# z^T for the gated block: turned by VectorE and read back through DRAM, in place of TensorE transposes

## The chip, the core and the metric

The kernel runs on one core of a Trainium2 chip. The metric is the device time of one execution in microseconds (us); times of several executions are given as a median. The engines are named as in the profile: PE is TensorE, PEld its weight loads, DVE is VectorE, ACT is ScalarE, POOL is GpSimd, SP is SyncE, which issues most of the loads.

## What is computed

A row block x of 2048 x 512 (float32) goes through four layers, each added to its input:

```
for layer in range(4):
    n = layernorm(x)
    if layer % 2 == 0:                       # mix: real part of a 2-D DFT
        a, b = n @ hid_re.T, n @ hid_im.T
        x = x + seq_re @ a - seq_im @ b
    else:                                    # gated block, F = 1792
        x = x + (gelu(n @ w_gate) * (n @ w_up)) @ w_down
```

## The kernel before

**Products.** Every float32 operand is split into a high and a low part (`split`, line 109: ScalarE copies with rounding, VectorE subtracts), and one product is three matmuls (`mm3`, lines 142 to 146: high by high, high by low, low by high). The larger products are done with seven half-size products in place of eight, in the scheme of Strassen and Winograd; the names A11 to A22, S1 to S4, B11 to B22 and T1 to T4 are those of its blocks and sums.

**SBUF and PSUM.** SBUF is cut into 102 slots of 128 x 512 (`Slots`, line 85), taken from the front of a list and put back at its end; PSUM into 8 tiles. A slot that is taken again waits for the last reader of its earlier content.

**Streamed weights.** The DFT matrices (`ws`, `wh`) and the split w_down (`wd`) come as a list of items in the order of use. `take` (line 221) hands out the next one. Before it does, it splits items up to AHEAD = 5 further on, and `split_next` (line 214) loads up to RAW = 4 beyond that. Loads go to SP's queue. For w_down the item is a pair of loads of halves that are already split, and the "split" does nothing (`lambda *w: w`, line 356).

**Steps on the side.** Work that is not a product is put into a list, `queue` (line 359), and `step` runs one entry after each item of the mix, after each item of the down product, and, while `making` holds, before each product of the gated block. In the first mix the queue first holds the norms and differences of layer 0, and then `down_weight_steps` (line 693) for the 14 pieces of w_down: a load on SP, a split, two stores of the halves on POOL, with two empty steps after each.

The instruction order in the built program is set by a scheduler that works from this order; within an engine the order is fixed then, SP's and POOL's queues too.

**The mix** (`mix`, line 507) goes over four blocks of 512 columns; in each come S2, S3 and A22 products with the sequence matrices and then the products with `wh`, after which a block of x is stored.

**The gated block** (`geglu`, line 728) makes two passes (w = 0, 1) over 1024 rows. A pass needs z^T, the normed rows turned, as eight blocks. `block_steps` (line 441) makes them: `norm(i)` for eight tiles of rows (`normed`, line 368), then for each of four column chunks and two parts `turned` (line 450), which transposes four 128 x 128 pieces on TensorE into a PSUM tile:

```
for i in range(NT):
    nc.tensor.transpose(ps[:, i * P:(i + 1) * P], z[part * NT + i][:, c * P:(c + 1) * P], ident)
```

`first` and `second` copy that tile with ScalarE, split it, and form differences T1, T2, T3. For the first pass these steps are queued at S3 of the last block of the mix (line 606), for the second pass after the first half of the down products of the first (line 876). Before the last stage of a mix everything left in the queue is run.

**Gate and up weights.** In the first pass of layer 1 the 14 pieces of w_gate and w_up are loaded raw (`weight_steps`, line 654: one load of 256 KB, two of 128 KB), summed, split and stored; the load, the sums and four splits are six steps of the queue. Pieces 0 and 1 are made at the end of the mix (lines 593 and 608), piece 2 at the start of the pass (line 860), piece n + 3 after pass n (line 827). Later passes load the split pieces (`weight_load`, line 709).

`up(n, ...)` (line 791) does the seven products of piece n, and between them matmuls of the down product that lags LAG = 6 pieces behind; `down` does the rest of the down products, 12 matmuls an item.

Of the kernel before, what the change touches and what calls it, by code (L numbers as in the profile page):

```python
# [14 lines left out]
P = 128  # L15
# [13 lines left out]
LAG = 6  # L29
EARLY = 2  # L30
# [8 lines left out]
def fnet_geglu(ctx: ExitStack, tc: tile.TileContext, x_in, ws, wh, wgu, wdn, out):  # L39
# [174 lines left out]
    def split_next():  # L214
        n = stream["split"]
        while stream["loaded"] <= min(n + RAW, len(items) - 1):
            load_next()
        parts[n] = items[n][2](*raws.pop(n))
        stream["split"] += 1

    def take():
        n = stream["used"]
        while stream["split"] <= min(n + AHEAD, len(items) - 1):
            need = items[stream["split"]][3]
            if need and need not in cs and stream["split"] > n:
                break
            split_next()
# [10 lines left out]
    def as_is(v):  # L238
        return (v,)

# [112 lines left out]
    for layer in range(0, 4, 2):  # L353
        mix_items(layer)
        for _ in range(NB // 2):
            items.extend((F32R, halves(wds[f]), lambda *w: w, None) for _ in range(2) for f in range(NF))
# [84 lines left out]
    def block_steps(layer, w):  # L441

        z, t = {}, {}

        def norm(i):
            def run():
                z[i] = normed(layer, w * 2 * NT + i)
            return run

        def turned(c, part):  # L450

            ps = ps8.get()
            for i in range(NT):
                nc.tensor.transpose(ps[:, i * P:(i + 1) * P], z[part * NT + i][:, c * P:(c + 1) * P], ident)  # L454
            if c == ND - 1:
                sb.put(*(z.pop(part * NT + i) for i in range(NT)))
            return ps
# [6 lines left out]
        def first(c):  # L464
            def run():
                ps = turned(c, 0)
                t[f"B{1 + c // 2}1", c % 2] = copied(ps)
                blocks[f"B{1 + c // 2}1", c % 2] = split_slot(ps)
                ps8.put(ps)
            return run  # L470

        def second(c):
            def run():
                ps = turned(c, 1)
                if c < 2:
                    t["B12", c] = copied(ps)
                    t["T1", c] = difference(ps, t["B11", c])
                    sb.put(t.pop(("B11", c)))
                else:
                    c0 = c - 2  # L480
                    t["T2", c0] = difference(ps, t["T1", c0])
                    t["T3", c0] = difference(ps, t["B12", c0])
                    sb.put(t.pop(("B12", c0)))
                    blocks["B22", c0] = split_slot(ps)
                ps8.put(ps)
# [14 lines left out]
        one = [norm(i) for i in range(NT)] + [first(c) for c in range(ND)]  # L500
        two = [norm(i) for i in range(NT, 2 * NT)] + [second(c) for c in range(ND)]
        two += [fourth(c) for c in range(2)]
        two += [divide(name, c) for name in ("T2", "T3", "T1", "T4") for c in range(2)]
        return one + two


    def mix(layer):
# [73 lines left out]
        chains, sides, us, ws4 = {}, {}, {}, {}  # L581

        def s2(b):
# [7 lines left out]
            sides[b] = side  # L591
            if last and layer == 0:
                queue.extend(weight_steps(0))
# [8 lines left out]
        def s3(b):  # L602
            last = b == NB - 1
            chain, side, u, w4 = chains[b], sides.pop(b), us.pop(b), ws4.pop(b)
            if last:
                queue.extend(block_steps(layer + 1, 0))
                if layer == 0:
                    queue.extend(weight_steps(1))
# [45 lines left out]
    def weight_steps(n):  # L654
# [36 lines left out]
        return [load, sums] + [divide(i) for i in range(len(pieces))]  # L691

    def down_weight_steps(f):

        raw = []

        def load():
            raw.append(sb.get())
            with tc.issue_after(stream["last"].ins):
                nc.sync.dma_start(raw[0], wdn[f])  # L700

        def store():
            p = plain(raw[0])
            kept(wds[f], p)
            sb.put(*p)

        return [load, store]
# [20 lines left out]
    def geglu(w, layer):  # L728
# [33 lines left out]
        making = layer == 1 and w == 0  # L762
# [28 lines left out]
        def up(n, down):  # L791
            product(n, chain[n], "S2", "T2", False, True)
# [33 lines left out]
            if making and n + 3 < NF:  # L826
                queue.extend(weight_steps(n + 3))
            elif not making and n + 2 < NF:
# [30 lines left out]
        if making:  # L859
            queue.extend(weight_steps(2))  # L860
# [7 lines left out]
        if before_mix:  # L868
# [115 lines left out]
```

## Time and profile before

| | |
|---|---|
| median of 3 runs | 1662.34 us (1661.48 to 1665.74) |
| profiled execution | 1666.76 us |
| its span, first to last instruction | 1664.9 us |
| granted TensorE clock, mean | 0.998 |
| DMA, moved in all | 388.46 MB, 233 GB/s |
| stores by POOL's queue | 57.16 MB |
| instructions | 22527 |

How to read it: a line L144 is line 144 of the kernel; "p" is a PSUM tile, "s" a slot of SBUF, both without their numbers. A group's row gives its count, busy time and mean duration in ns, and then the idle time of the engine before it with what ended it. A row of a windows view gives, for a stretch of the span, the busy time of each engine with the number of instructions, the granted clock and the share of the DMA engines' time. A row of DMA issues gives the count, the size and the median time from issue to landing. In the chain of waits each piece is followed back from the end to what released it.

### The profile page before, as it was taken

How to read it: one execution, taken by the hardware profiler on the slowest of the kernel's cores; microseconds unless marked ns; L12 is line 12 of the kernel's file. 1: busy time of each engine (PE TensorE's matmuls, PEld its weight loads, DVE VectorE, ACT ScalarE, POOL GpSimd, SP SyncE). 2: the span in 40 equal slices, each digit the busy share in tenths (PEclk: the TensorE clock that was granted, in tenths of full speed). 3: DMA queues.
4: the chain of work that ended last, by engine and by line, in shares of the span. 5: the costliest groups of instructions: out<-in, count | busy, mean ns of one | idle time of the engine just before them, and what ended most of it. 6: DMA issues, size and time to landing. Idle time of an engine off the chain costs nothing.

```text
span 1664.9 us, 22527 instructions
## 1 busy us (share of the span) xinstructions
PE 1650.4 (99%) x7296; PEld 1359.2 (82%) x7296; DVE 1190.7 (72%) x2132; ACT 776.2 (47%) x1352; POOL 169.3 (10%) x288
## 2 busy tenths in 40 slices
PE   9999999999999999999999999999999999999999
PEld 6877788888788888888888888888888888888887
DVE  8997978687887765655898785857946556656561
ACT  7744434255565543534663333444635443444440
POOL 3212100021422110000210000000100000100000
PEclk9999999999999999999999999999999999999999
DMA  9788886778766876555665766565695559755551
GB/s 361 247 279 329 306 317 227 253 252 291 273 229 215 292 269 233 172 189 198 216 227 182 240 228 228 168 227 188 225 386 184 171 177 321 259 178 175 186 183 51
DMA packets 200726, 388.46 MB, mean 233 GB/s; under 512 B 23840, under 2 KB 27424, under 8 KB 200608
## 3 DMA queue, kind: packets, MB, share of 16 engines
q1 hardware_dynamic: 183168, 329.86, 59.1%
q0 software_dynamic: 17440, 57.16, 9.1%
q8 instruction: 58, 0.95, 0.2%
q14 instruction: 60, 0.49, 0.1%
HBM read 328.73 MB, written 58.20 MB: 232 GB/s over the span
## 4 chain that ended last, share of the span: by engine, by line
PE 93%; DVE 3%; DMA 2%; issue 1%; ACT 1%; SPq 0%; DVEq 0%; ACTq 0%
PE p L144 31%; PE p L145 30%; PE p L146 30%; DMA s<-wgu 2%; DVE s L111 1%; PE p L551 1%; PE p L454 1%; DVE s L135 1%; DMA s<-ws 1%; DVE s L132 1%; DMA s<-x 0%; DVE s L725 0%; DVE s L739 0%; DVE s L723 0%; ACT s L110 0%
## 5 line engine op out<-in xcount | busy, mean ns | idle before, releaser
L145 PE MATMUL p<-s,s 128*128 128x512 f32 x2368 | 921.7, 390 | 1.9 <-DVE s L111 1.9
L146 PE MATMUL p<-s,s 128*128 128x512 f32 x2368 | 908.6, 390 | 0.0
L144 PE MATMUL p<-s,s 128*128 128x512 f32 x2368 | 901.2, 391 | 7.0 <-DVE s L135 3.9
L110 ACT ACTIVATE s<-s 128x512 fp32r<-128x512 f32 (+1 forms) x758 | 438.0, 617 | 467.6 <-DVE s L132 98.6
L111 DVE TENSOR_TENSOR s<-s,s 128x512 fp32r<-128x512 f32 (+1 forms) x758 | 490.2, 679 | 87.1 <-ACT s L110 64.3
L144 PEld LDWEIGHTS p<-s,s 128*128 128x128 f32 x2368 | 445.0, 188 | 102.9 <-DVE s L135 5.0
L145 PEld LDWEIGHTS p<-s,s 128*128 128x128 f32 x2368 | 445.4, 188 | 95.0 <-DVE s L111 3.1
L146 PEld LDWEIGHTS p<-s,s 128*128 128x128 f32 x2368 | 445.2, 188 | 93.7 <-DVE s L111 0.7
L135 DVE TENSOR_TENSOR s<-s,p 128x512 f32<-128x512 f32 x316 | 213.0, 685 | 188.9 <-PE p L146 140.6
L139 ACT ACTIVATE s<-p 128x512 f32<-128x512 f32 x248 | 145.2, 593 | 187.4 <-PE p L146 171.4
L132 DVE TENSOR_TENSOR s<-s,s 128x512 f32<-128x512 f32 (+1 forms) x290 | 172.4, 608 | 23.4 <-DMA s<-ws 15.4
L722 ACT ACTIVATE s<-s 128x512 f32<-128x512 f32 x112 | 70.4, 630 | 91.7 <-DVE s L135 90.9
L725 DVE SCALAR_TENSOR_TENSOR s<-s,s 128x512 f32<-128x512 f32 x112 | 76.8, 690 | 38.2 <-ACT s L724 37.6
L378 POOL TENSOR_TENSOR rstd<-rstd,power 128x1 f32<-128x1 f32 x64 | 50.8, 803 | 506.7 <-DVE rstd L377 500.8
L723 DVE SCALAR_TENSOR_TENSOR s<-s,s 128x512 f32<-128x512 f32 x112 | 77.0, 690 | 33.5 <-ACT s L722 31.3
L724 ACT ACTIVATE s<-s 128x512 f32<-128x512 f32 x112 | 69.5, 627 | 25.0 <-DVE s L723 24.4
L135 DVE TENSOR_TENSOR s<-s,s 128x512 f32<-128x512 f32 (+1 forms) x78 | 50.1, 645 | 38.5 <-DMA s<-ws 22.1
L169 POOL DMA_DIRECT2D x<-s x48 | 26.1, 543 | 443.8 <-DVE s L135 440.8
L382 ACT ACTIVATE s<-s,shift,rstd 128x512 f32<-128x512 f32 x64 | 50.4, 811 | 36.5 <-DVE shift L380 32.1
L739 DVE SCALAR_TENSOR_TENSOR s<-s,s 128x512 f32<-128x512 f32 x84 | 58.0, 690 | 1.6
L197 POOL DMA_DIRECT2D wb<-s x84 | 45.2, 540 | 121.6 <-ACT s L110 85.1
L373 DVE BATCH_NORM_STATS2 st<-s 128x6 f32<-128x512 f32 x64 | 42.7, 689 | 19.8 <-DMA s<-x 19.8
(32 smaller groups left out, 254.6 us busy)
## 6 DMA issues: line engine op xcount, KB each, us to landing
s<-ws SPq DMA_DIRECT2D x432, 256.0 KB, 4.0
s<-wb SPq DMA_DIRECT2D x294, 256.0 KB, 4.1
s<-wd SPq DMA_DIRECT2D x224, 256.0 KB, 4.3
s<-x SPq DMA_DIRECT2D x126, 256.0 KB, 4.1
s<-wh SPq DMA_DIRECT2D x120, 256.0 KB, 4.8
wb<-s POOLq DMA_DIRECT2D x98, 256.0 KB, 3.5
x<-s POOLq DMA_DIRECT2D x48, 256.0 KB, 4.1
wd<-s POOLq DMA_DIRECT2D x28, 256.0 KB, 4.9
```

The lines of the kernel that those rows point to most:

```text
L110: nc.scalar.activation(hi, src, AF.Copy)
L111: nc.vector.tensor_tensor(lo, src, f32(hi), op=ALU.subtract)
L132: nc.vector.tensor_tensor(out, a, b, op=ALU.subtract)
L135: nc.vector.tensor_tensor(out, a, b, op=ALU.add)
L139: nc.scalar.activation(v, src, AF.Copy)
L144: nc.tensor.matmul(ps, ah, bh, start=start, stop=False, skip_group_check=True)
L145: nc.tensor.matmul(ps, ah, bl, start=False, stop=False, skip_group_check=True)
L146: nc.tensor.matmul(ps, al, bh, start=False, stop=stop, skip_group_check=True)
L722: nc.scalar.activation(t, g, AF.Square)
L723: nc.vector.scalar_tensor_tensor(t, t, 1.0 / GELU_C, g, op0=ALU.add, op1=ALU.mult)
L724: nc.scalar.activation(t, t, AF.Tanh, scale=GELU_A * GELU_C)
L725: nc.vector.scalar_tensor_tensor(t, t, 1.0, g, op0=ALU.add, op1=ALU.mult)
```

## The change

z^T is no longer made by TensorE. Each normed tile is turned by VectorE, whose transpose turns blocks of 32 x 32 in place, and the result is stored to DRAM by POOL's queue (`turned`, two tensors of 512 x 512 for a pass). `fetch(c)` then reads each of the eight blocks back with four loads on SP's queue, which put the 32 x 32 blocks where they belong: 32 partitions, in each 16 runs of 32 numbers. `first` and `second` use the slot that was read; the copies out of PSUM are gone.

The norms stand in the queue on their own now: those of a gated block's first pass from S2 and S3 of the next to last block of the mix on, each with an empty step after it; the rest of `block_steps` at S3 of the last block as before. For a second pass all of it is queued six down products earlier.

`weight_steps` gives back the raw load apart from the sums and splits. It is issued a piece earlier: those of pieces 0 and 1 at S2 of the last block, that of piece 2 at the start of the pass, and that of piece n + 3 when pass n begins, while the sums and splits of piece n + 2 are queued.

`down_weight_steps` is gone. In the first use of w_down the item is the raw piece; `make_down_first` splits it and stores the halves. Items of w_down that are already split are loaded and handed on at most NEAR = 2 items ahead in each of the two stages.

```diff
+NEAR = 2
     def split_next():
         while stream["loaded"] <= min(n + RAW, len(items) - 1):
+            if stream["loaded"] > n + NEAR and items[stream["loaded"]][2] is whole:
+                break
             load_next()
     def take():
+            if items[stream["split"]][2] is whole and stream["split"] > n + NEAR:
+                break
             split_next()
+    def make_down_first(f):
+        def run(v):
+            p = plain(v)
+            kept(wds[f], p)
+            return p
+        return run
-            items.extend((F32R, halves(wds[f]), lambda *w: w, None) for _ in range(2) for f in range(NF))
+                    if layer == w == part == 0:
+                        items.append((F32, (wdn[f],), make_down_first(f), None))
+                    else:
+                        items.append((F32R, halves(wds[f]), whole, None))
         def norm(i):
             def run():
-                z[i] = normed(layer, w * 2 * NT + i)
+                z, v = normed(layer, w * 2 * NT + i), sb.get()
+                nc.vector.transpose(v, z)
+                part, n = divmod(i, NT)
+                nc.gpsimd.dma_start(turned[part][n * P:(n + 1) * P], v)
+                sb.put(z, v)
-        def turned(c, part):
-            ps = ps8.get()
-            for i in range(NT):
-                nc.tensor.transpose(ps[:, i * P:(i + 1) * P], z[part * NT + i][:, c * P:(c + 1) * P], ident)
+        def fetch(c):
+            def run():
+                for part in range(2):
+                    v = zt[c, part] = sb.get()
+                    for i in range(P // 32):
+                        cols = turned[part][:, c * P + i * 32:c * P + (i + 1) * 32]
+                        to = v[i * 32:(i + 1) * 32]
+                        nc.sync.dma_start(
+                            to.rearrange("p (j t) -> p j t", t=32), cols.rearrange("(j p) t -> p j t", p=32)
+                        )
         def first(c):
-                ps = turned(c, 0)
-                t[f"B{1 + c // 2}1", c % 2] = copied(ps)
-                blocks[f"B{1 + c // 2}1", c % 2] = split_slot(ps)
+                v = t[f"B{1 + c // 2}1", c % 2] = zt.pop((c, 0))
+                blocks[f"B{1 + c // 2}1", c % 2] = split_slot(v)
...
+            if b == NB - 2:
+                norms, others = block_steps(layer + 1, 0)
+                queue.extend([run for norm in norms[:NT] for run in (norm, None)])
+                rest.extend((norms[NT:], others))
             if last and layer == 0:
-                queue.extend(weight_steps(0))
+                opening_weights.update((n, weight_steps(n)) for n in range(2))
+                queue.extend([opening_weights[0][0], None, opening_weights[1][0], None, *opening_weights[0][1]])
...
         def up(n, down):
+            if n + 3 in making:
+                making[n + 3][0]()
+            if n + 2 in making:
+                queue.extend(making[n + 2][1])
...
-            if making and n + 3 < NF:
-                queue.extend(weight_steps(n + 3))
...
-            queue.extend(block_steps(layer, 1))
...
-    for run in [run for f in range(NF) for run in down_weight_steps(f)]:
-        queue += [run, None, None]
```

More of the change, by code (lines that the diff above doesn't have):

```diff
@@ L689, in divide @@
             return run
[L691 to L707, printed above, removed]
+        return load, [sums] + [divide(i) for i in range(len(pieces))]
     def weight_load(n):
@@ L867, in geglu @@
         load_rows(0)
-        if before_mix:
+        if w == 0:
+            queue.extend(run for part in block_steps(layer, 1) for run in part)
+        elif before_mix:
             queue.extend((lambda k=k: first_rows(layer + 1, k)) for k in range(NK))
```

51 lines of the change are left out of this document (28 added, 23 removed).

## The prediction

> **What bounds the kernel now.** First the page: span, engines, and the chain that ended last.
>
> ```profile
> span 1664.9 us, 22527 instructions
> ...
> PE 1650.4 (99%) x7296; PEld 1359.2 (82%) x7296; DVE 1190.7 (72%) x2132; ACT 776.2 (47%) x1352; POOL 169.3 (10%) x288
> ...
> PE 93%; DVE 3%; DMA 2%; issue 1%; ACT 1%; SPq 0%; DVEq 0%; ACTq 0%
> ```
>
> TensorE is busy in 99% of the span, and it makes up 93% of the chain. So only two things can move the end: work taken off TensorE, and stalls of TensorE. Next its timeline at transposes that go away:
>
> ```profile
> 1194.92 0.39 PE L144 MATMUL p<-s,s 128*128 128x512 f32 x1
> 1195.15 0.39 PE L145 MATMUL p<-s,s 128*128 128x512 f32 x1
> 1195.38 1.91 PE L454 MATMUL p<-ident,s 128*128 128x128 f32 x16
> 1197.04 0.48 PE L146 MATMUL p<-s,s 128*128 128x512 f32 x1
> 1197.36 0.40 PE L144 MATMUL p<-s,s 128*128 128x512 f32 x1
> ```
>
> The durations of 0.39 us overlap: matmuls start 0.23 us apart (1194.92, 1195.15, 1195.38), and that spacing, 0.227 us, is the price of one. From 1195.38 to 1197.36 run sixteen transposes and one matmul: 1.98 less 0.23 is 1.75 us, 0.109 us a transpose. Then where TensorE stands still, by stage:
>
> ```profile
> core 0: us, PE busy (x) PEld busy (x) DVE busy (x) ACT busy (x) POOL busy (x), PEclk, DMA share, GB/s
> 70.00:140.00 70.00, 67.48 (x295) 54.88 (x295) 66.61 (x112) 33.45 (x60) 10.80 (x20) 1.00 0.78 265
> 140.00:210.00 70.00, 67.70 (x293) 55.60 (x292) 61.28 (x100) 31.12 (x55) 16.18 (x30) 0.98 0.91 337
> 260.00:300.00 40.00, 40.00 (x178) 33.13 (x177) 30.57 (x50) 17.94 (x30) 1.05 (x2) 1.00 0.67 230
> 300.00:336.00 36.00, 36.00 (x161) 29.80 (x160) 27.37 (x46) 9.76 (x16) 1.07 (x2) 1.00 0.71 230
> 336.00:372.00 36.00, 34.98 (x156) 28.59 (x155) 31.52 (x64) 18.88 (x32) 7.29 (x13) 1.00 0.75 259
> 432.00:452.00 20.00, 17.12 (x67) 13.13 (x66) 14.42 (x30) 9.79 (x20) 5.38 (x10) 0.91 0.70 251
> 1041.00:1080.00 39.00, 39.00 (x173) 32.28 (x172) 32.32 (x54) 16.64 (x29) 0.54 (x1) 1.00 0.51 173
> ```
>
> TensorE idles where VectorE is at 88 to 95% (70 to 210, and 336 to 372) and at the opening of layer 1 (432 to 452). A stall costs more than its length:
>
> ```profile
> 200.64 0.39 PE L145 MATMUL p<-s,s 128*128 128x512 f32 x1
> 203.33 0.80 PE L144 MATMUL p<-s,s 128*128 128x512 f32 x1 [2.30 <-DVE s L135]
> 203.92 0.63 PE L145 MATMUL p<-s,s 128*128 128x512 f32 x1
> 204.34 0.63 PE L146 MATMUL p<-s,s 128*128 128x512 f32 x1
> ```
>
> After 2.3 us of rest the next matmuls start 0.43 us apart (203.92, 204.34), seven or so of them: some 1.6 us more.
>
> **The transposes go.** Line 454 stands 16 times in each part of a pass: 2 layers by 2 passes by 2 parts by 16 are 128. At 0.109 us: **-14.0 us**, all on the path. Their copies (24 of L139) and the splits out of PSUM only relieve ScalarE and VectorE, which lie beside.
>
> **What VectorE gets.** 32 transposes of 128x512, as large as a tensor_tensor. No row shows one; the nearest are these.
>
> ```profile
> L132 DVE TENSOR_TENSOR s<-s,s 128x512 f32<-128x512 f32 x200 | 136.2, 691 | 19.0 <-DMA s<-ws 15.4 <-PE p L146 1.7 <-issue 0.8
> ...
> L373 DVE BATCH_NORM_STATS2 st<-s 128x6 f32<-128x512 f32 x64 | 42.7, 689 | 19.8 <-DMA s<-x 19.8
> ...
> L375 DVE BATCH_NORM_AGGREGATE mv<-st 128x2 f32<-128x6 f32 x64 | 10.3, 176 | 0.1
> L380 DVE SCALAR_TENSOR_TENSOR shift<-mv,rstd 128x1 f32<-128x1 f32 x64 | 9.9, 158 | 11.6 <-POOL rstd L378 11.1
> L377 DVE TENSOR_SCALAR rstd<-mv 128x1 f32<-128x1 f32 x64 | 8.2, 151 | 0.4
> L132 DVE TENSOR_TENSOR s<-s 128x256 f32<-128x256 f32 x16 | 6.7, 425 | 0.0
> L135 DVE TENSOR_TENSOR s<-s,s 128x256 f32<-128x256 f32 x14 | 6.0, 425 | 16.3 <-DMA s<-wgu 13.4 <-PE p L146 2.8
> ```
>
> From 0.43 us (the half row) to 1.4 us (two passes of the full row); I take 0.69. For the first pass of a layer, eight norms move out of the crowded end of the mix into its block 2. Each brings 0.69 + 0.18 + 0.15 + 0.16 + 0.69 = 1.9 us of VectorE: 15 us into 260 to 336, where it is busy 57.9 of 76. That just fits in layer 0. In layer 2 the stretch from 1041 is at 83% already (32.32 of 39), four norms add 7.5 us there, and in the changed program's order several loads of that place are released only 10 to 25 matmuls (2.3 to 5.7 us) before the first matmul that hangs on them. A load lands after 4 us (below) and its sums and splits take 2 more, so one stall of some 3 us with its slow matmuls: **+4 us** (0 to 8).
>
> Each transpose is followed by a store on POOL's queue, and the next norm's power stands behind that store, which waits for the transpose. POOL is busy 10%, a step lies between two norms, and only the reads much later need the stores: at nothing. Without that room, a norm would be late by the length of one transpose.
>
> **The opening and the first pass of layer 1.** The fourteen loads and splits of w_down leave the queue that runs from 85 to 212 us: 14 times 0.69 = 10 us less for VectorE just where it is full, and 28 stores less on POOL's queue. The rests there are 2.52 + 2.30 = 4.8 us, with slow matmuls some 6. I count half: **-3 us** (0 to -6). In 432 to 452 the rest is 2.9 us, with slow matmuls 4.5; there the raw weights (SP's loads of wgu, on which VectorE's sums wait, 13.4 us in the L135 row) come a pass earlier, and the norms are done. Half again: **-2 us** (0 to -4.5). The w_down splits now fall one to a pair of products (12 us) from 490 on; 0.69 us of VectorE each at about 80% load, and they also save 28 loads. At nothing, hidden under matmuls; without that cover at most 14 times 0.69.
> Split weights are held only two items ahead; an item of the down product is 12 matmuls, 2.7 us, so loads still lead by four or five items, 11 to 13 us, against 4 to 5 to land: nothing.
>
> **Reading z^T back.** Here the change adds a wait. Each pass issues 32 reads on SP's queue, each 32 partitions by 16 runs of 128 bytes: 64 KB in 512 runs, 32 for each of 16 engines. SP is in order, so what stands behind them, weights for the mix or for the down products, waits, and the matmuls wait for those.
>
> ```profile
> q1 hardware_dynamic: 183168, 329.86, 59.1%
> ...
> s<-ws SPq DMA_DIRECT2D x432, 256.0 KB, 4.0
> ...
> s<-wgu SPq DMA_DIRECT2D x14, 256.0 KB, 4.7
> s<-wgu SPq DMA_DIRECT2D x28, 128.0 KB, 3.4
> ```
>
> ```profile
> 370.81 1.28 SPq L210 DMA_DIRECT2D s<-wh  x3
> ```
>
> No row has such runs. From below: SP issues three loads in 1.28 us, each 0.33 long, so one per 0.47 us; that is a floor. From above: a 128-byte run costs as much as a packet of now, 59.1% of 16 engines by 1664.9 us over the 183,168 packets of q1 = 0.086 us, or 2.8 us a read. By bytes alone it would be a quarter of a 256 KB load (8 packets an engine, 0.7 us), under the floor. The wgu rows decide the choice: with half the bytes in as many packets the landing falls from 4.7 to 3.4 us, so bytes count for much. I take **0.5 us**.
> What that must fit into comes from the changed program's order. Before layer 1, 27 reads stand between matmul 1449, which frees the slots, and a weight load that matmul 1550 hangs on: 101 matmuls are 22.9 us, less 4 to land and 2 to split leaves 17, 0.63 us a read. Before the second pass of layer 1, all 32 come after matmul 2539, and matmul 2653 needs the last: 25.8 us, less the landing and the last differences, 19 us or 0.6 a read. In layer 3 it is looser: some 0.9, and 1.0 (two groups of 16). So at 0.5 us all are covered, with little left; I charge **+2.5 us** for crowding with other traffic.
>
> The Trainium skill, "VectorE: DVE Perf Modes", section "The three transpose paths", speaks against the change: it warns that a plain DMA that transposes by strides is 19 times slower than the 1309 ns of the crossbar for 128x128 elements; as an estimate that is 24 ns an element on each of 16 engines, and as much for each run here would make 0.8 us a read, at which the second case below begins. No run here shows it yet.
>
> **Sum.** -14.0 + 4 - 3 - 2 + 2.5 = -12.5 us. The profiled execution took 1666.8 us (span 1664.9), so it would take 1654.3; the median of the runs shown, 1662.34, is 4.4 lower, and with it the forecast is **1650**. A measurement of this kernel tells about 0.3%, 5 us, from no change.
>
> **Rivals.**
> *The reads hold the queue (slower).* One mechanism: 128-byte runs cost by the run, SP's queue stands behind the 32 reads, and TensorE waits for weights or blocks after each group. At 1.0 us a read the first group is late by 27 x 0.37 = 10 us, the second by 32 x 0.4 = 13, the third by 3; with four cold starts of 1.6 us that is 32 us: 1682. At 1.5 us it is 24 + 29 + 19 + 8 + 6 = 86: about 1736. It decides from about 0.8 us a read, where 27 x 0.17 = 5, 32 x 0.2 = 6 and two cold starts, 14 us in all, eat the gain: 1664. For it: nothing in the trace moves in such runs, and the slack of the first two groups is small. Against: the wgu rows, and DMA engines that rest a quarter of 336 to 372.
> *VectorE takes back what TensorE gave (no change).* Transposes at 1.4 us make 15 us into 21 in block 2, more than the 18 that are free; both layers stall there (4 to 8 us each), and the opening keeps its stalls: 1662. For it: every rest of TensorE today ends with VectorE or ScalarE. Against: with transposes at 0.69 us the 18 us hold them.
> *The change doesn't do what it says:* the transposes are gone from TensorE's order, so this keeps no chance.
>
> **Chances.** Forecast 0.46; reads hold the queue 0.44, of which 0.38 beyond 0.85 us a read, from 1668 up, and 0.06 about the break-even; VectorE takes it back 0.10. The forecast's own range is 1640 (all rests of the three stages gone, no new ones) to 1657. Eight in ten must reach into the second case, up to 1.0 us a read and a little past it: 1640 to 1692. So faster 0.46, same 0.16 (0.06 + 0.10), slower 0.38.
>
> **What would show it.** Right: no transposes on PE, no rest of over 2 us at the four groups of reads, reads 0.5 us apart on SP, and rests at 80 to 210 and 432 to 452 halved. Wrong: reads landing later and later in a group, TensorE ended by a DMA or a split of ws or wd behind them, PE's clock falling there; or transposes of over 1 us on VectorE with rests in block 2.

## The result and the profile after

The changed kernel takes **1681.26 us** (median of 4 runs, 1675.84 to 1684.24) against 1662.91 us (1661.48 to 1665.74) for the kernel before: 1.0105 times as long, interval 1.0075 to 1.0134. The forecast was 1650; the time lies inside the range of 1640 to 1692 and on the other side of no change. The profiled execution took 1684.24 us.

The page of the changed kernel, and two rows of its DMA issues (count, KB each, median us from issue to landing):

```profile
span 1682.5 us, 22457 instructions
...
PE 1649.1 (98%) x7168; PEld 1352.3 (80%) x7168; DVE 1205.5 (72%) x2164; ACT 766.1 (46%) x1328; POOL 189.8 (11%) x320
...
q1 hardware_dynamic: 246720, 330.91, 61.7%
```

```profile
t<-s POOLq DMA_DIRECT2D x32, 256.0 KB, 5.2
s<-t SPq DMA_DIRECT2D x128, 64.0 KB, 2.8
```

```profile
L393 DVE BATCH_NORM_STATS2 st<-s 128x6 f32<-128x512 f32 x64 | 42.6, 688 | 30.6 <-DMA s<-x 30.5
...
L470 DVE STREAM_TRANSPOSE s<-s 128x512 f32<-128x512 f32 x32 | 22.3, 704 | 4.0 <-ACT s L402 4.0
```

TensorE has 128 instructions less, and the span is 17.6 us longer. So TensorE lost over 30 us elsewhere. Where, the view by stretches shows (PE busy, then the other engines, granted clock, DMA share, GB/s); all but 372 to 400, 860 to 890, 1080 to 1090 and 1455 to 1485 are stretches that the prediction showed of the kernel before:

```profile
70.00:140.00 70.00, 67.87 (x298) 55.60 (x297) 65.97 (x111) 33.41 (x59) 5.93 (x11) 1.00 0.70 232
140.00:210.00 70.00, 70.00 (x310) 57.98 (x309) 57.58 (x95) 27.58 (x49) 8.06 (x15) 1.00 0.78 261
260.00:300.00 40.00, 37.69 (x165) 30.56 (x164) 34.53 (x72) 21.01 (x35) 7.65 (x13) 1.00 0.72 233
300.00:336.00 36.00, 32.33 (x135) 26.22 (x135) 27.24 (x46) 11.91 (x19) 1.14 (x2) 0.95 0.92 305
336.00:372.00 36.00, 33.50 (x141) 27.12 (x140) 32.34 (x57) 15.53 (x29) 5.90 (x11) 0.95 0.83 209
372.00:400.00 28.00, 24.90 (x98) 18.71 (x97) 26.11 (x43) 16.81 (x31) 0.54 (x1) 0.94 0.84 276
432.00:452.00 20.00, 20.00 (x90) 16.57 (x89) 17.90 (x34) 12.92 (x24) 7.79 (x16) 1.00 0.86 294
860.00:890.00 30.00, 26.51 (x104) 20.96 (x103) 28.85 (x51) 18.86 (x35) 1.12 (x2) 0.89 0.69 222
1041.00:1080.00 39.00, 39.00 (x174) 32.30 (x173) 29.13 (x50) 11.49 (x19) 3.02 (x5) 1.00 0.64 202
1080.00:1090.00 10.00, 7.20 (x24) 4.98 (x23) 9.81 (x26) 8.23 (x15) 3.86 (x6) 0.83 0.47 158
1455.00:1485.00 30.00, 24.61 (x94) 19.19 (x93) 19.35 (x31) 12.07 (x21) 2.16 (x4) 0.89 0.96 298
```

140 to 210 and 432 to 452 are full now; 260 to 336, which was full before, is not, and neither are four more stretches that were full. Before they read:

```profile
372.00:400.00 28.00, 28.00 (x141) 23.52 (x140) 23.69 (x52) 20.41 (x37) 3.21 (x5) 1.00 0.87 295
860.00:890.00 30.00, 30.00 (x134) 24.85 (x133) 27.61 (x47) 14.71 (x27) 1.12 (x2) 1.00 0.71 238
1080.00:1090.00 10.00, 10.00 (x46) 8.28 (x45) 7.07 (x12) 7.22 (x13) 0.00 (x0) 1.00 0.48 148
1455.00:1485.00 30.00, 30.00 (x135) 24.82 (x134) 18.27 (x28) 14.54 (x25) 0.00 (x0) 1.00 0.55 186
```

Below, all kernels are compared by the **lost time** of TensorE: from the start times of its instructions in the trace, how much later each starts than its usual distance after the one before it (0.227 us after a matmul, 0.109 after a transpose, 0.170 after the warm-up matmuls at the start and 0.430 after those on operands that are not split, both in the first 31 us alone; differences under 0.03 us are left out). Rests and the slow matmuls behind them both count. In us:

| | in all | 70-210 | 255-330 | 330-410 | 410-460 | 560-665 | 860-910 | 1060-1150 | 1420-1500 |
|---|---|---|---|---|---|---|---|---|---|
| before | 19.9 | 7.3 | 0 | 1.7 | 5.2 | 0.3 | 0 | 0 | 0.5 |
| after | 49.2 | 2.6 | 8.4 | 10.5 | 0 | 2.3 | 6.7 | 5.0 | 9.0 |

29.3 us more lost, less 14.0 us for the transposes, make 15.3 of the 17.6 us; the differences below the threshold make 2.0 of the rest. (The first 70 us lose 3 to 4 us in every kernel; they are in the total and in none of the columns.)

Three of the new places, in the trace of the changed kernel. VectorE in block 2 of layer 0, at an early norm:

```profile
301.50 0.69 DVE L393 BATCH_NORM_STATS2 st<-s 128x6 f32<-128x512 f32 x1 [2.26 <-DMA s<-x]
```

VectorE stood for 2.26 us at a norm whose row had not landed, and the splits and sums for the mix stood behind it, in order. TensorE waited for such a sum:

```profile
306.38 0.50 PE L145 MATMUL p<-s,s 128*128 128x512 f32 x1 [3.67 <-DVE s L136]
```

SP's queue at the first group of reads (L484 is a read, L211 a load of streamed weights; start, length of the row, count):

```profile
351.63 2.60 SPq L484 DMA_DIRECT2D s<-t  x4
354.40 1.47 SPq L211 DMA_DIRECT2D s<-ws  x1
355.91 0.43 SPq L484 DMA_DIRECT2D s<-t  x1
356.44 0.43 SPq L211 DMA_DIRECT2D s<-ws  x1
356.92 7.36 SPq L484 DMA_DIRECT2D s<-t  x13
364.33 0.49 SPq L211 DMA_DIRECT2D s<-ws  x1
364.86 7.98 SPq L484 DMA_DIRECT2D s<-t  x14
372.88 6.58 SPq L211 DMA_DIRECT2D s<-ws  x11
379.82 10.97 SPq L211 DMA_DIRECT2D s<-wh  x14
```

Thirteen reads in 7.36 us and fourteen in 7.98 are 0.57 us a read. In 21 us from 351.6 to 372.8 three loads of weights get through; then 25 follow one behind the other, all of 256 KB, and TensorE catches up with them at the end:

```profile
391.88 0.47 PE L145 MATMUL p<-s,s 128*128 128x512 f32 x1 [2.29 <-DMA s<-wh]
```

In these 18 us SP does not issue all the time: for 9.4 us it waits, mostly for slots. The load that landed just before 391.88 was issued at 388.06, after a wait of 1.79 us. So the length of the clump and the scarcity of slots are not separated at this stall.

### The profile page after: what moved, and what is told of

It reads as the page before. It is cut to its first block, busy times and chain, and to the rows that moved or that the text cites. A ratio compares the mean times of both kernels' runs of the same rounds, so it can differ in the third digit from the quotient of the medians.

```text
span 1682.5 us, 22457 instructions
## 1 busy us (share of the span) xinstructions
PE 1649.1 (98%) x7168; PEld 1352.3 (80%) x7168; DVE 1205.5 (72%) x2164; ACT 766.1 (46%) x1328; POOL 189.8 (11%) x320
## 3 DMA queue, kind: packets, MB, share of 16 engines
q1 hardware_dynamic: 246720, 330.91, 61.7%
q0 software_dynamic: 20000, 65.55, 10.3%
## 5 line engine op out<-in xcount | busy, mean ns | idle before, releaser
L145 PE MATMUL p<-s,s 128*128 128x512 f32 x2368 | 897.4, 392 | 17.5 <-DVE s L136 10.2
L111 ACT ACTIVATE s<-s 128x512 fp32r<-128x512 f32 (+1 forms) x782 | 453.5, 617 | 521.6 <-DVE s L133 111.9
L112 DVE TENSOR_TENSOR s<-s,s 128x512 fp32r<-128x512 f32 (+1 forms) x782 | 506.6, 682 | 124.8 <-ACT s L111 93.5
L145 PEld LDWEIGHTS p<-s,s 128*128 128x128 f32 x2368 | 446.8, 189 | 115.8 <-ACT s L111 13.4
L146 PEld LDWEIGHTS p<-s,s 128*128 128x128 f32 x2368 | 447.6, 189 | 105.4 <-DVE s L112 10.8
L133 DVE TENSOR_TENSOR s<-s,s 128x512 f32<-128x512 f32 (+1 forms) x314 | 189.2, 617 | 40.0 <-DMA s<-ws 18.7
L140 ACT ACTIVATE s<-p 128x512 f32<-128x512 f32 x224 | 130.6, 591 | 133.9 <-PE p L147 132.8
L136 DVE TENSOR_TENSOR s<-s,s 128x512 f32<-128x512 f32 (+1 forms) x78 | 50.4, 646 | 37.5 <-DMA s<-ws 23.3
L393 DVE BATCH_NORM_STATS2 st<-s 128x6 f32<-128x512 f32 x64 | 42.6, 688 | 30.6 <-DMA s<-x 30.5
```

Source lines behind the costliest of these rows:

```text
L111: nc.scalar.activation(hi, src, AF.Copy)
L112: nc.vector.tensor_tensor(lo, src, f32(hi), op=ALU.subtract)
L133: nc.vector.tensor_tensor(out, a, b, op=ALU.subtract)
L136: nc.vector.tensor_tensor(out, a, b, op=ALU.add)
L140: nc.scalar.activation(v, src, AF.Copy)
L145: nc.tensor.matmul(ps, ah, bh, start=start, stop=False, skip_group_check=True)
```

## The experiments

The theory after this reading: the price of a read was right, but its cover was not; the norms in block 2, the short lead of two items and the backlog behind the reads each make TensorE wait. The rivals: that the reads would cost the same on any queue or be harmless if their bytes moved otherwise, and that the new stalls come from a single part. Fourteen kernels were run. Each is compared with the kernel before on the same chip, which took 1665.3 us (e1 to e4), 1666.4 (e5 to e7), 1665.8 (e8 to e11) and 1666.2 (e12 to e14).

| run | us | ratio to before, interval | lost in all | 255-330 | 330-410 | 410-460 | 560-665 | 860-910 | 1060-1150 | 1170-1250 | 1420-1500 |
|---|---|---|---|---|---|---|---|---|---|---|---|
| e1 | 1667.34 | 1.0010 (1.0000-1.0019) | 19.9 | 0 | 8.6 | 3.3 | 0.6 | 0 | 0 | 0.4 | 0.3 |
| e2 | 1698.08 | 1.0194 (1.0170-1.0219) | 64.1 | 0 | 19.3 | 0 | 5.5 | 6.2 | 0 | 17.2 | 5.7 |
| e3 | 1707.46 | 1.0252 (1.0229-1.0276) | 69.2 | 5.3 | 12.0 | 0.1 | 17.9 | 6.9 | 7.3 | 6.3 | 7.2 |
| e4 | 1673.00 | 1.0044 (1.0028-1.0059) | 37.1 | 8.2 | 9.6 | 0 | 1.9 | 0 | 6.8 | 1.4 | 1.9 |
| e5 | 1659.57 | 0.9965 (0.9953-0.9978) | 13.8 | 0 | 2.4 | 0.7 | 2.4 | 0 | 0 | 0.4 | 0.2 |
| e6 | 1674.65 | 1.0053 (1.0032-1.0073) | 36.9 | 10.5 | 3.8 | 0 | 7.2 | 0 | 5.6 | 0.6 | 1.4 |
| e7 | 1707.71 | 1.0257 (1.0240-1.0275) | 72.2 | 11.4 | 12.5 | 2.4 | 10.8 | 0 | 18.7 | 1.2 | 7.8 |
| e8 | 1667.59 | 1.0011 (1.0001-1.0021) | 20.4 | 0 | 6.5 | 2.8 | 0.3 | 0 | 0 | 0.4 | 0.5 |
| e9 | 1658.16 | 0.9951 (0.9936-0.9967) | 12.8 | 0 | 1.2 | 0.1 | 2.3 | 0 | 0 | 0.4 | 1.6 |
| e10 | 1669.35 | 1.0023 (1.0011-1.0035) | 35.6 | 10.3 | 5.4 | 0 | 6.1 | 0.7 | 4.6 | 0 | 1.5 |
| e11 | 1673.22 | 1.0052 (1.0036-1.0069) | 36.2 | 10.3 | 6.6 | 0 | 7.7 | 0 | 2.8 | 0.4 | 2.5 |
| e12 | 1668.51 | 1.0012 (1.0002-1.0022) | 18.4 | 3.6 | 4.8 | 0 | 0.6 | 0 | 1.3 | 0.4 | 0.5 |
| e13 | 1692.69 | 1.0165 (1.0148-1.0182) | 58.5 | 0 | 20.0 | 0 | 9.7 | 0 | 0 | 17.6 | 2.4 |
| e14 | 1679.24 | 1.0089 (1.0074-1.0104) | 31.6 | 0 | 6.7 | 8.6 | 0.4 | 5.1 | 0 | 0.3 | 0.5 |

The lost time is that of one profiled execution, the time a median; they agree within some 6 us.

### e1: everything but the turning

The changed kernel with TensorE's transposes and the norms' old places back: the earlier raw weights and the w_down split at first use stay, NEAR = 2 too.

```diff
-                nc.vector.transpose(v, z)
...
+                nc.tensor.transpose(ps[:, i * P:(i + 1) * P], z[part * NT + i][:, c * P:(c + 1) * P], ident)
```

> TensorE transposes and the old places of the norms are put back into the changed kernel; the earlier raw weights and w_down split at first use stay. Theory (the reads' hold on SP's queue and the early norms cost the time, the rest of the change gains): no stalls of TensorE over 2 us at 200 and 440, none at 260-310, 360-395 and 1460-1480; 1652 us, 10 below before. Rival (the w_down part with its short lead costs): the stalls about 870 and 1083 stay and the time is 1662 or more.

The gains at 70 to 210 came, and as much was lost again at 330 to 410 and 410 to 460; the sum is no change. The theory's 1652 us missed; the rival's 1662 or more came, but not by the stalls at 870 and 1083 that it named, which are gone. The largest stall:

```profile
354.98 0.76 PE L145 MATMUL p<-s,s 128*128 128x512 f32 x1 [3.75 <-DVE s L136]
```

So the parts around the turning were not worth what they seemed: one of them costs about 7 us at this place. No stall stands at 860 to 910 or 1420 to 1500, so NEAR = 2 by itself does not make those.

### e2: the norms late

The changed kernel with all of `block_steps` queued at S3 of the last block.

```diff
-                queue.extend([run for norm in norms[:NT] for run in (norm, None)])
...
-                queue.extend(rest[1])
+                queue.extend(run for part in block_steps(layer + 1, 0) for run in part)
```

> The changed kernel with the norms of a gated block's first pass back at S3 of the last block, reads and turning by VectorE kept. Theory (early norms crowd VectorE in block 2): the stalls at 260-310 (8 us) and 1083 (5 us) go, those behind the reads stay; 1668 to 1672 us. Rival (the norms have to be early for the reads): the reads come so late that TensorE waits for the blocks; 1690 us or more.

The stalls at 255 to 330 and 1060 to 1150 are gone, so they belong to the early norms. But, as the rival had it, 19.3 us are lost at 330 to 410 and 17.2 at 1170 to 1250, the last with this stall:

```profile
1240.11 1.22 PE L145 MATMUL p<-s,s 128*128 128x512 f32 x2 [6.57 <-ACT s L111]
```

Norm, transpose, store, read and split stand one behind the other, on VectorE, ScalarE, POOL's queue and SP's; in the changed kernel the store alone lands after 5.2 us and the read after 2.8. With that chain the norms have to be early.

### e3: the reads on ScalarE's queue

```diff
-                        nc.sync.dma_start(
+                        nc.scalar.dma_start(
```

> The changed kernel with the 128 reads of z^T issued by ScalarE's queue and not by SP's; the same runs on the same DMA engines. Theory (the reads hold SP's queue, and the weight loads behind them come in a clump): stalls at 360-395 and 1460-1480 fall by more than half; 1664 to 1670 us, with some 64 us more of issuing on ScalarE. Rival (the 128-byte runs load the DMA engines, whoever issues them): 1681 us, as changed.

Much worse than theory and rival had it, and by one stall above all: ScalarE's queue at the second group of reads (26 of them in 26 us), and TensorE behind it.

```profile
620.49 26.35 ACTq L484 DMA_DIRECT2D s<-t  x26
646.89 3.23 ACT L111 ACTIVATE s<-s 128x512 fp32r<-128x512 f32 x6 [36.57 <-DMA s<-wb]
```

```profile
647.57 1.22 PE L145 MATMUL p<-s,s 128*128 128x512 f32 x2 [15.82 <-ACT s L111]
```

A read takes 1 us of this queue here, and 0.65 to 1 at the first group, where it takes 0.57 of SP's (why was not taken apart), and the engine that splits stands behind all of them. Which queue issues the reads decides who waits; the hold does not go away.

### e4: the lead of the w_down items

```diff
-NEAR = 2
+NEAR = 9
```

> The changed kernel with NEAR = 9, so that split w_down is loaded and held as far ahead as in the kernel before. If the short lead makes the stalls about 870 and 1083: they go, 1670 us. If they come from the early norms and the slots these hold: no change, 1678 to 1684 us.

8.3 us faster than the changed kernel by the medians, 10 by the ratios; 860 to 910 is clean and 1420 to 1500 goes from 9.0 to 1.9. The stall at 1083, which the forecast put to the short lead too, stays (6.8 us at 1060 to 1150). The same stretches as above:

```profile
860.00:890.00 30.00, 30.00 (x134) 24.86 (x133) 28.79 (x49) 17.22 (x32) 1.12 (x2) 1.00 0.81 258
...
1455.00:1485.00 30.00, 28.63 (x125) 23.08 (x124) 24.51 (x41) 15.86 (x28) 2.16 (x4) 1.00 1.02 365
```

At 1455 to 1485 the DMA engines are busier (1.02 against 0.96) and TensorE waits less: more was on its way. The order of the list gives a reason: items are loaded in turn, so layer 2's first matrices cannot be loaded past the last w_down items, which NEAR = 2 holds back. But e1 has that order and that limit too, and no such stall: the short lead costs only beside the turning by VectorE (see e8).

### e5: the w_down split alone

The kernel before with w_down split at its first use and NEAR = 9; nothing else of the change.

```diff
-            items.extend((F32R, halves(wds[f]), lambda *w: w, None) for _ in range(2) for f in range(NF))
+                        items.append((F32, (wdn[f],), make_down_first(f), None))
...
+                        items.append((F32R, halves(wds[f]), whole, None))
-    for run in [run for f in range(NF) for run in down_weight_steps(f)]:
-        queue += [run, None, None]
```

> The kernel before with one part of the change alone: w_down split at first use (lead as before, NEAR = 9). Theory: the stalls at 200 (4 us) and part of those at 80 to 130 go, VectorE has room for the splits later; 6 us below before (a ratio of 0.996 to 0.998). Rival (the splits come back as stalls in layer 1): within 2 us of before.

Faster than both kernels: 0.9965, some 5.8 us. Not only the opening is better; 410 to 460 loses 0.7 us where it lost 5.2:

```profile
430.00:460.00 30.00, 30.00 (x134) 24.83 (x133) 29.42 (x58) 21.51 (x42) 13.51 (x26) 1.00 0.81 289
```

### e6: the reads earlier and spread

The changed kernel with NEAR = 9 and the reads in eight groups of four, with an empty step after each, from S2 of the last block.

```diff
-        two = [fetch(c) for c in range(ND)] + [first(c) ...
+            if last:
+                queue.extend([run for read in reads for run in (read, None)])
```

> The changed kernel with NEAR = 9 and, for a gated block's first pass, the reads in eight groups of four with an empty step between, from S2 of the last block of the mix on; the same number of reads at the same price. Theory (a clump of reads holds SP's queue for 17 to 21 us, and what stands behind it comes in a clump): the stalls at 340 to 400 (9 us with NEAR = 9) and the 1.4 us at 1214 go; 1664 us, 9 below the run with NEAR = 9. Rival (the reads cost wherever they stand): 1673 us, as with NEAR = 9.

330 to 410 goes from 9.6 us (e4) to 3.8, as the theory of the backlog has it, and 1170 to 1250 to 0.6. But 255 to 330 and the second pass of layer 1 give it back (10.5 for 8.2, 7.2 for 1.9), and the time is no better than e4's. In the second passes the edit makes eight steps of reads out of four, so these are not as in e4. The forecast of this run missed: it took the other stalls as fixed.

### e7: the short runs on the store's side

NEAR = 9, and each tile stored with four stores of 128-byte runs on POOL, so that a block is read back with one plain load of 256 KB.

```diff
-                nc.gpsimd.dma_start(turned[part][n * P:(n + 1) * P], v)
+                for a in range(P // 32):
+                    nc.gpsimd.dma_start(cols.rearrange("(j p) t -> p j t", p=32), v[a * 32:(a + 1) * 32]...)
```

> The changed kernel with NEAR = 9, and the 128-byte runs moved to the store's side: each turned tile goes out in four stores on POOL's queue that put the 32 x 32 blocks in place, and SP reads each block of z^T with one load of 128 rows of 2 KB, 8 loads for a pass in place of 32. Theory (the number of reads on SP's queue costs): stalls at 340 to 400 and 1460 to 1480 fall below 3 us together; 1663 us, 10 below the run with NEAR = 9. Rival (the 128-byte runs cost on the DMA engines, on whichever side): 1673 us or more.

Worse by 35 us than e4. The theory looked at SP alone; the stores now hold POOL:

```profile
267.41 7.78 POOL L474 DMA_DIRECT2D t<-s  x12 [1.26 <-DVE s L470]
```

Twelve stores hold POOL for 7.8 us, 0.65 each. That this makes the 35 us is not shown: the next power of a norm in this view stands at 293.27, 18 us behind these stores, and waited for VectorE. The loss is spread over the columns of the table and was not taken apart.

### e8: the earlier raw weights

The kernel before with the w_down split (e5) and the raw weights a piece earlier; NEAR = 9.

```diff
-                queue.extend(weight_steps(0))
+                queue.extend([opening_weights[0][0], None, opening_weights[1][0], None, *opening_weights[0][1]])
```

> The kernel before with the earlier raw weights and the w_down split at first use, NEAR = 9; the transposes stay on TensorE. Theory, the earlier raw weights cost: the stalls at 340-355 us that the run with NEAR = 2 showed (7.0 us) stay, since a short lead cannot make them, and the time is 1665 to 1668 us. Rival, the short lead of two items cost what that run lost: the stalls go, and the time is that of the w_down edit alone, 1659 to 1661 us.

As the theory had it: 1667.59, and against e5 the stalls of e1 are back (6.5 and 2.8 us). Between e5 and e8 only the raw weights differ: 1.0011 against 0.9965, 7.7 us. What they take shows in SP's queue. In e5, behind the raw loads of the first piece, eight loads of matrices follow:

```profile
324.12 16.01 SPq L211 DMA_DIRECT2D s<-ws  x8
```

and in e8, behind two of these:

```profile
328.74 0.33 SPq L685 DMA_DIRECT2D s<-wgu  x1
329.16 0.38 SPq L686 DMA_DIRECT2D s<-wgu  x1
329.59 0.42 SPq L687 DMA_DIRECT2D s<-wgu  x1
333.23 6.72 SPq L211 DMA_DIRECT2D s<-ws  x5
```

The second piece's three raw loads stand where e5 goes on with matrices, and the next load of a matrix, which waits for a slot, is issued at 333.23. Counted by its place among the loads of ws, the 206th is issued at 328.70 in e5 and at 333.23 in e8, the 214th at 346.13 and 351.60. The piece's sums stand on VectorE at 335 and its stores on POOL at 393 to 406, so its slots are held that long; in e5 it is loaded only at 400. From 340.3 on VectorE of e8 does not rest until behind the sum for which TensorE stands still at 354.96 (3.75 us), so what delays that sum is VectorE's order; how much of it comes from the late loads and how much from the piece's own sums was not taken apart.

e8 settles one thing more. It differs from e1 in NEAR alone, 9 for 2, and the two take 1.0011 and 1.0010 of the kernel before: with TensorE's transposes the short lead costs nothing.

### e9: VectorE turns for the second passes only

e5, and the changed kernel's `block_steps` (here `turned_steps`) for w = 1 alone, queued where the changed kernel queues it; the first pass keeps TensorE's transposes.

```diff
-            queue.extend(block_steps(layer, 1))
...
+            queue.extend(turned_steps(layer, 1))
```

> The kernel before with the w_down split at first use (NEAR = 9) and the turning by VectorE in the second pass of each geglu layer only; the first pass keeps TensorE's transposes and the norms' old places. Theory, early norms and first-pass reads make the loss: 64 transposes leave TensorE (-7.0 us from 1659.6), the stalls of the two second passes come (2.2 and 1.9 us with NEAR = 9): 1655 to 1658 us, and nothing new stands at 260-400 and 1080 us. Rival, the reads hold SP's queue wherever they are: the second passes stall by 8 us or more, and the time is 1661 us or more.

**The fastest of all**: 1658.16 us, 0.9951 (0.9936 to 0.9967). The reads hold SP's queue as long as anywhere, and hardly anybody waits (TensorE once, 0.89 us at 628):

```profile
604.11 19.49 SPq L550 DMA_DIRECT2D s<-t  x32
623.70 1.05 SPq L211 DMA_DIRECT2D s<-wd  x2
624.85 29.89 SPq L806 DMA_DIRECT2D s<-wb  x34
```

```profile
600.00:630.00 30.00, 29.11 (x129) 23.77 (x128) 13.68 (x23) 8.35 (x16) 2.55 (x5) 1.00 0.90 215
630.00:660.00 30.00, 30.00 (x134) 24.83 (x133) 24.56 (x40) 17.43 (x31) 0.00 (x0) 1.00 0.86 313
```

Its profiled span is 6.7 us shorter than e5's, what 64 transposes are worth (7.0), but the medians of the two lie only 1.4 us apart, with intervals that overlap. That e9 beats both kernels is measured; that it beats e5 is not.

### e10 and e11: norms spread, rows asked for ahead

e10 is e6 with one norm in six steps over the whole of block 2, its x row asked for four steps before. e11 is the same without the earlier raw weights.

```diff
-        one = [norm(i) for i in range(2 * NT)]
+        one = [run for i in range(2 * NT) for run in (ask(i), None, None, None, norm(i), None)]
```

> The changed kernel with NEAR = 9, the reads in eight groups of four from S2 of the last block, the norms of the rows ahead one in six steps over the block before it, and each x row asked for four steps before its norm. Theory, VectorE's norm that stands waiting for its x row makes the stalls at 300 and 1078 us (7.7 and 3.4 us with the reads spread alone): they go to under 3 us together, and the time is 1664 to 1668 us. Rival, they come from the slots and the queue's backlog whatever the norm waits for: 1672 to 1677 us.

> The same spreading of norms, x rows and reads, with VectorE turning in both passes, but the raw weights asked for where the kernel before asks for them. Theory, the earlier raw weights fill the same stretch as the reads: without them the stretch 340-400 us has under 4 us of stalls, and the time is 1652 to 1658 us, below the 1659.6 of the w_down edit alone. Rival, the turning costs what it frees whatever stands beside it: 1660 to 1667 us.

e10 is the best with VectorE in both passes, some 1 us above its forecast, but the stalls that it aimed at are still there (10.3 and 4.6 us where the theory had under 3 together). VectorE in e10:

```profile
302.92 0.71 DVE L470 STREAM_TRANSPOSE s<-s 128x512 f32<-128x512 f32 x1 [0.88 <-ACT s L402]
307.65 0.69 DVE L393 BATCH_NORM_STATS2 st<-s 128x6 f32<-128x512 f32 x1 [4.03 <-DMA s<-x]
```

and the load of that row in SP's queue:

```profile
300.50 0.96 SPq L211 DMA_DIRECT2D s<-wh  x2
302.29 0.32 SPq L163 DMA_DIRECT2D s<-x  x1
```

To ask for a row earlier in the order does not bring it earlier: SP issues in order, what stands ahead of it waits for slots, and the row was issued at 302.3 and landed 5 us later. e11 missed its forecast of 1652 to 1658 by 15 us: the earlier raw weights, which cost 7.7 us beside TensorE's transposes, are worth 4 to 5 us beside VectorE's (3.9 by the medians, 4.8 by the ratios). Without them their loads come at S2 and S3 of the last block, together with the reads; that this is why was not shown.

### e12: the norms twice

e5, and beside it the eight norms of each first pass computed once more where the changed kernel computes them.

```diff
+            if b == NB - 2:
+                queue.extend(run for i in range(NT) for run in (lambda i=i: sb.put(normed(layer + 1, i)), None))
```

> The kernel before with the w_down split at first use (NEAR = 9), which ran in 1659.6 us with no stall over 1.6 us after 130 us, and beside that the eight norms of the rows ahead computed once more where the changed kernel computes them (block 2, one in two steps), their results thrown away; nothing is turned, stored or read back by VectorE. Theory, the norms themselves at that place make the stalls at 260-310 and 1080 us, since they stand in VectorE's and ScalarE's order waiting for their x rows: stalls of 4 to 9 us at 260-310 and 2 to 5 us near 1080, 1666 to 1672 us. Rival, the transposed tiles and their stores do it (they hold slots until the stores have landed): under 2 us at both places, 1659 to 1662 us.

The time is the theory's (1668.5), the places only in part: 3.6 us at 255 to 330, where the changed kernel loses 8.4, 1.3 at 1060 to 1150 for 5.0, and 2.4 more than e5 at 330 to 410 (4.8). Norms alone, with no tile turned or stored, cost 4.6 us of lost time and some 8 us in the medians (0.0047). What of the rest is the transposes' and what the stores', which hold a slot each for 5 us, was not taken apart.

### e13: the norms in the last block

e5 with VectorE in both passes; for the first the norms in S2 of the last block, the reads spread over S3.

```diff
+            if last:
+                queue.extend(run for n, norm in enumerate(norms) for run in (norm, others[n] ...))
```

> VectorE turns in both passes; raw weights where the kernel before asks for them; w_down split at first use with NEAR = 9; for the first pass the norms stand in S2 of the last block (one in two steps), the reads in S3 in eight groups of four (one group in two steps), the sums behind them. Theory, block 2 was the wrong place (raw matrices loaded with little lead there) and the last block the right one as long as the reads are spread: no stall at 300 and 1080 us, under 4 us in 340-440 us, 1652 to 1657 us, below the 1658 us of turning the second pass alone. Rival, the last block's stretch is where the reads, the matrices and the raw weights meet: 8 us or more of stalls in 360-440 and 1100-1240 us, 1662 us or more.

The rival, and more: 20.0 us at 330 to 410 and 17.6 at 1170 to 1250. The largest stall of layer 2:

```profile
1210.44 0.79 PE L145 MATMUL p<-s,s 128*128 128x512 f32 x1 [9.04 <-ACT s L140]
```

So the early place of the norms, dear as it is, is the better one of the three that were tried (block 2, S2 and S3 of the last block). Which of norms, reads and matrices makes these 37.6 us was not taken apart.

### e14: five slots less

```diff
-NSLOT = 102
+NSLOT = 97
```

> The kernel before with the w_down split at first use (NEAR = 9), and 97 SBUF slots in place of 102; nothing else. Theory, what the early norms take is slots, and the raw matrices' loads in 260-400 and at 870 and 1080 us start as late as slots come free: with five fewer, stalls of 8 us or more in all at those places, 1667 us or more. Rival, the slots are not what is short there, it is VectorE's and SP's order: under 3 us of new stalls, 1660 to 1662 us.

e5 with 97 slots: 1679.24 us, 20 us slower than with 102. So slots are scarce here, as the theory had it; the places are not all those it named. Nothing stands at 255 to 330 or 1060 to 1150; 330 to 460 and 860 to 910 lose 20.4 us. The first is the place of e1 and e8:

```profile
355.67 0.50 PE L145 MATMUL p<-s,s 128*128 128x512 f32 x1 [3.01 <-DVE s L136]
```

That the earlier raw weights (four slots a piece, held through part of the last block) cost by their slots fits this and SP's queue in e8. 860 to 910 loses 5.1 us here with the long lead and without the turning, so a stall there takes no short lead if slots are short. For the early norms fewer slots alone do not make the place (0 at 255 to 330): there the norms stand in VectorE's order (e12, and the wait of 4.03 us in e10), together with loads that SP issues late.

## Why the prediction was wrong

By differences between kernels that differ in one part (ratio times 1664 us):

| part | from | us |
|---|---|---|
| w_down split at first use, long lead | e5 to before | -5.8 |
| raw weights a piece earlier | e8 to e5 | +7.7 |
| VectorE turns for the second pass | e9 to e5 | -2.3 (not told from 0) |
| VectorE turns for the first pass, norms early | e4 to e8, less the line above | +7.8 |
| NEAR = 2 in place of 9 | after to e4 | +10 |

They add up to the 17.5 us that 1.0105 stands for but for rounding, as they must, since each was taken where the one before left off; in another order they would be other numbers. The last line above all: without the turning the short lead costs 0 (e1 to e8), so its 10 us are those of NEAR = 2 beside the turning, and with the short lead the turning costs 15.8 us (after to e1), with the long one 5.5 (e4 to e8).

Point by point:

- **The transposes go, -14.0.** Right; 7296 less 7168 are the 128, and the lost time accounts for the span with them.
- **A transpose on VectorE, 0.69 us.** Right: 0.704. The rival in which VectorE takes back by 1.4 us a transpose is out.
- **Norms in block 2 of layer 0, "just fits", at nothing.** Wrong: 8.4 us. The step compared VectorE's free time with the norms' busy time. It left out that VectorE works in order and that each norm waits on it for a row from SP's queue. The row of BATCH_NORM_STATS2 says it: its idle time went from 19.8 to 30.6 us. The norms also hold slots for which SP's loads wait: between 255 and 312 us of the changed kernel two of these waits, 3.7 us, end with a norm's step on ScalarE. With the norms late nothing is lost there (e2); with the norms alone, nothing turned or stored, 3.6 us (e12). So more than half of the 8.4 seems to hang on the turning and its stores; how was not taken apart.
- **The stores on POOL's queue, at nothing.** Nothing speaks against it: VectorE waits for POOL's powers for 8.9 us in all, 11.1 before.
- **Layer 2, +4.** Right in place and size: 5.0 us at 1083. The reason fits in part: e2, with the norms late, loses 0 there, and VectorE works without a rest from 1069 to 1088; that loads came too late was not shown.
- **The opening, -3, and 432 to 452, -2.** Right in sign and too small: -4.7 and -5.2. The reason for the second was wrong. It was put to the earlier raw weights; e5 has the gain without them (0.7 left), and e8 with them has less of it (2.8). The w_down split at first use brings it; by which of its loads, splits and stores was not taken apart.
- **The earlier raw weights' own cost** stands nowhere in the sum. e8: +7.7 us.
- **NEAR = 2: "loads still lead by four or five items ... nothing".** Wrong for this kernel, about 10 us (after to e4), and right without the turning (e1 to e8). The lead was worked out for w_down items between other w_down items. At the end of a pass and before layer 2 the items behind them cannot be loaded past them; why that hurts only beside the turning stays open. Neither the early norms nor reads on SP's queue are needed for it: e2 and e3, each without one of the two and with NEAR = 2, still lose 6.2 and 6.9 us at 860 to 910.
- **A read at 0.5 us.** Nearly right: 0.57 to 0.61, far from the 2.8 of the upper bound and below the 0.8 at which the first rival decides. A run of 128 bytes costs an engine (61.7% of 1682.5 us less 59.1% of 1664.9) times 16 over 63,552 more packets = 14 ns; the packets of 128 bytes in the trace, 65,536 of them, took 13.4 ns each. The Trainium skill, "VectorE: DVE Perf Modes", section "The three transpose paths", warns of a plain DMA that transposes by strides, 19 times slower than the crossbar when the innermost stride of the destination is large; from it 0.8 us a read had been estimated. These reads write runs of 32 numbers in a row and are not that case: a run costs less here than the 24 ns estimated for one element.
- **"So at 0.5 us all are covered, with little left; I charge +2.5."** The step that failed at the reads. The budget was that of the first load behind each group. Behind the first group stood 25 loads, and TensorE waited at the end of that clump, 19 us after the last read was issued; e6, which spreads the reads, has 3.8 us there for e4's 9.6 (and no better time). Of the 10.5 and 9.0 us lost at 330 to 410 and 1420 to 1500, the second was mostly NEAR's (1.9 left in e4).
- **The rival "reads hold the queue"** named 1682 at 1.0 us a read. The time is near that, the mechanism is not: the reads cost 0.57, and in the second pass of layer 1, where it saw 13 us, e9 has 20 us of reads on SP and TensorE waiting for 0.89. So it is luck that 1681 lies within the range, which reached that far for a price of a read that did not come.

So the forecast failed on three terms set at nothing or left out (early norms; NEAR, which costs beside the turning; raw weights) and one too small (the backlog), and on none of the prices of an operation.

## What to carry to other kernels

A step that is moved must be checked against the order of every queue it joins and the buffers it holds, not against an engine's free time: 15 us of work into 18 us of room cost 8 us. Behind a group of DMAs on an in-order queue count the whole backlog until the lead is made up, and ask what a limit on lookahead keeps out behind the items that it limits. Parts of a change that come together should be priced alone where they can be: here one of them, with a longer lead, was worth 5.8 us, and the whole lost 18. And a price found so holds beside the parts that it was found with: the same short lead cost 0 and 10 us.

## What the hardware showed that was not expected

Runs of 128 bytes are cheap to read by SP's queue: 64 KB in 512 of them landed after 2.8 us, against 4.0 for the 256 KB of a load of ws in 2 KB runs, and were issued 0.57 us apart. The same runs as stores on POOL's queue (e7) take 0.65 us of POOL each. On ScalarE's queue (e3) 26 such reads took 26 us, and ScalarE ran nothing of its own for 36.57 us.
